# Linear attention ahead of two expert layers: one product of every third token tile moved to VectorE, one decayed copy of k left out, and the heads put together by wider products

## The chip, the cores and the metric

One core of a Trainium2 chip runs the whole program. The metric is the device time of one execution in microseconds (us); three executions of the kernel before were timed, and one more was profiled. Engines are named as in the profile: PE is TensorE's matmul, PEld its weight loads, DVE VectorE, ACT ScalarE, POOL GpSimd, SP SyncE.

## The reference

Four sequences of 768 tokens, eight heads, 48 numbers per head. A state per head takes in `k v` of each token and decays by `w`; a token also sees its own `k v`, weighted by `u`:

```python
for t in range(S):
    cur = einsum('bhd,bhe->bhde', u[None] * k[:, :, t], v[:, :, t])
    y[:, :, t] = einsum('bhd,bhde->bhe', r[:, :, t], state + cur)
    state = w[None, :, :, None] * state + einsum('bhd,bhe->bhde', k[:, :, t], v[:, :, t])
x = y.transpose(0, 2, 1, 3).reshape(B * S, H * D)      # 3072 tokens of 384
e_idx = argmax(x @ w_gate); gate_w = softmax(x @ w_gate)[e_idx]; eom = sigmoid(x @ w_output_gate)
out[e_idx == e] = gate_w * eom[:, e] * (relu(x @ w1[e]) @ w2[e])
return (silu(out @ moe2_w_gate) * (out @ moe2_w_val)) @ moe2_w_out
```

## The kernel before

The tokens are cut into 24 tiles of 128, six to a sequence. The first stage goes through the attention tile by tile; the second runs the eight experts on gathered tokens, the third the dense layer. The change is in the first stage, and in code that the kernel only branches to when a decay is out of its range (`sequential`, which does not run here).

Within a tile the decay becomes a product: `rdT` is r transposed times powers of w, `kdT` is k transposed over powers of w, and `kdc` is k by token, decayed to the tile's end. For tile i the engines do this:

- POOL, in `scaled_k(i)`: `ck` = k times u (L455), `ck` times r (L456), `kdT` (L458), `kdc` (L459). For the first three tiles the two products of `ck` are on DVE instead (L452, L453), with the intermediate in PSUM.
- DVE: `rdT` (L466), `cb`, the sum of `ck` over each head (L478), two masked copies of the scores into `dsb` (L499), the new state `st` (L527, or L522 for a sequence's first tile), and `lg`, the sum of router logits over the heads (L131).
- ACT: eight products that put `cb` on the diagonal of `dsb` (L482), the copy `yT` of the output (L556), then `xt` and `lh` out of `psx` (L126, L129).
- PE: the scores `pss` (L495), `pskv` for the state (L517, not for a sequence's sixth tile, which needs no next state), `psy` from `dsb` and v (L543) and from the state (L551), and `psx` (L124). `psx` multiplies `yT` by a table `unit`, which holds an identity and the router weights, so that one product gives x by token and the partial logits. The two heads of a pair lie in partitions 0 to 63 and 64 to 127, and a product takes 64 rows (one head) and 64 of the 128 tokens: 16 products of 64 columns per tile.

The loop `for i in range(NTILE + 3)` writes all of this out in one order, and PE, DVE, ACT, POOL and SP keep that order while it runs (their own schedules are switched off). In step i it issues `rdT` and `cb` of tile i + 1, the scores of tile i, the state of tile i - 1, `scaled_k(i + 2)`, the outputs of tile i - 1 and `psx` of tile i - 2. Between them `advance()` hands out one operation at a time of the routing of the sequence that is done (`route`, `gate`: mostly small DVE work), and `weights` splits expert weights early: `w1l` and `w2l` on DVE (L1063, 768 columns) in steps 12, 13, 15, 16, 18 and 19. Inputs come into a ring of three buffers, so `load(i + 3)` waits until DVE and POOL are done with tile i. The PSUM pools hold eight banks: `psx` has two of them, the scores two. After the loop the program works on the first expert's first tokens (`head`) while the last sequence is routed. Behind that a scheduler sets the order of the expert stage from its own estimate of times.

Of the kernel before, what the change touches and what calls it, by code (L numbers as in the profile page):

```python
# [38 lines left out]
def moe_kernel(ctx, tc, cst, small, tok, tr, u, w1, w2, m_gate, m_val, m_out, out):  # L39
# [76 lines left out]
    unit = const.tile([P, NP, 64], F32, name="unit")  # L116

    def emit(yT, x_rows, lg, pool, ps_x):
# [6 lines left out]
        xt = pool.tile([P, NP, 2, D], F32, name="xt")  # L125
        nc.scalar.copy(xt.rearrange("p q j d -> p j q d"), psx[:, :, 0:NP, 0:D])  # L126
        nc.sync.dma_start(out=x_rows, in_=xt.rearrange("p q j d -> p (q j d)"))
        lh = pool.tile([P, 2, NP, G], F32, name="lh")
        nc.scalar.copy(lh, psx[:, :, 0:NP, D:])  # L129
        yield  # L130
        nc.vector.reduce_sum(lg, lh.rearrange("p j q e -> p e (j q)"), axis=AX.X)  # L131
# [174 lines left out]
    with ExitStack() as actx:  # L306
# [111 lines left out]
        def units():  # L418
            for j in range(2):
                pr = slice(64 * j, 64 * j + 64)  # L420
                nc.gpsimd.tensor_copy(
                    unit[pr, :, 0:D],
                    ident[pr, 64 * j : 64 * j + D].rearrange("p (o d) -> p o d", o=1).to_broadcast([64, NP, D]),
                )
            nc.gpsimd.tensor_copy(unit[:, :, D:], wg[:, :, 0:G])

        S = {}
# [156 lines left out]
        def rows_out(i):  # L584
# [27 lines left out]
        with tc.manual_schedule(engines=set(engines)):  # L612
# [164 lines left out]
    def sequential(c):  # L777
# [8 lines left out]
        nc.vector.memset(ones, 1.0)  # L786
        lg = sq.tile([P, NTILE, G], F32, name="sq_lg")
        st = sq.tile([P, NP, D], F32, name="sq_st")
        with tc.For_i(0, B) as b:
            nc.vector.memset(st, 0.0)  # L790
            with tc.For_i(0, NCH) as ch:
# [709 lines left out]
```

## Time and profile before

| | |
|---|---|
| median of three executions | 829.43 us (829.01 to 830.25) |
| the profiled execution | 828.89 us, span 827.1 us, mean granted clock 0.991 |
| busy in the span | PE 790.2 us, DVE 515.1, ACT 347.6, POOL 210.6 |
| attention stage | from the start to 131.2 us, where `lg` of the last tile starts |

The span is the time from the first to the last instruction; 1.8 us of the execution lie outside of it. Busy shares are averages over stages with different limits: the attention stage must be read by itself.

### The profile page before, as it was taken

What the parts mean: (1) busy time and instruction counts of PE and PEld (TensorE: products, weight loads), DVE (VectorE), ACT (ScalarE), POOL (GpSimd) and SP (SyncE); (2) the same over time, 40 slices, a digit from 0 to 9 for tenths busy, and PEclk for the clock granted to TensorE, in tenths of its full rate; (3) what the DMA queues carried; (4) which work ended last, traced back from release to release, by engine and by line L of the source; (5) the groups of instructions that cost most, each with busy time, mean ns of one, the idle gap of its engine ahead of it and who ended that gap; (6) DMA issues with size and microseconds to landing.
All of it is one profiled execution on the core that took longest, in us unless ns stands there. A gap on an engine that the chain in (4) does not pass through costs nothing.

```text
span 827.1 us, 15617 instructions
## 1 busy us (share of the span) xinstructions
PE 790.2 (96%) x5982; PEld 718.5 (87%) x5983; DVE 515.1 (62%) x1091; ACT 347.6 (42%) x791; POOL 210.6 (25%) x207
## 2 busy tenths in 40 slices
PE   7989779699999999999999999999999999999997
PEld 4877678688999999998888888888888888889997
DVE  7789997399999999955554335333533443344443
ACT  5878663364575576554432222212222222122322
POOL 6999951354524422200001000200020020001000
PEclk9999999899999999999999999999999999999999
DMA  8899933686777877342210000000000010001000
GB/s 322 297 361 334 332 128 108 215 268 194 253 222 260 252 245 253 89 139 86 86 59 32 19 1 13 39 0 1 14 39 1 0 45 1 1 7 40 1 20 24
DMA packets 61860, 99.28 MB, mean 120 GB/s; under 512 B 5461, under 2 KB 48105, under 8 KB 61776
## 3 DMA queue, kind: packets, MB, share of 16 engines
q1 hardware_dynamic: 58320, 88.34, 32.3%
q0 software_dynamic: 3456, 9.85, 3.5%
q8 instruction: 49, 0.80, 0.4%
q14 instruction: 35, 0.29, 0.1%
HBM read 81.64 MB, written 16.53 MB: 119 GB/s over the span
## 4 chain that ended last, share of the span: by engine, by line
issue 58%; PE 16%; DVE 4%; POOL 3%; DMA 1%; ACT 1%; POOLq 0%; SPq 0%; ACTq 0%; DVEq 0%
PE ph L1188 7%; PE py L1188 6%; POOL out_dram L1332 2%; PE pya L1188 1%; DMA m<-ab 1%; PE pha L1188 1%; DVE w2l L1063 1%; PE pt L1154 1%; DVE ab L1034 1%; DMA cva<-in_w_gate_dram 0%; DVE exw L1027 0%; PE ph L1184 0%; DVE ab L1030 0%; DVE h L1208 0%; DVE low L1033 0%
## 5 line engine op out<-in xcount | busy, mean ns | idle before, releaser
L1361 DVE TENSOR_TENSOR hv<-pg,hv 128x512 f32<-128x512 f32 (+1 forms) x84 | 51.6, 615 | 153.8 <-ACT hv L1360 153.7
L1332 POOL DMA_INDIRECT out_dram<-ot,tokd x24 | 24.8, 1035 | 448.3 <-DVE ot L1331 443.6
L1360 ACT ACTIVATE hv<-pg 128x512 f32<-128x512 f32 (+1 forms) x84 | 45.1, 537 | 167.4 <-PE pg L1356 167.2
L966 ACT CAST hh<-hv 128x512 fp32r<-128x512 f32 (+1 forms) x84 | 47.0, 560 | 142.1 <-DVE hv L1362 142.1
L1323 PE MATMUL po<-wh,hl 128*128 128x384 f32 x288 | 96.8, 337 | 0.0
L1323 PE MATMUL po<-wh,hh 128*128 128x384 f32 x288 | 96.8, 336 | 0.0
L1323 PE MATMUL po<-wl,hh 128*128 128x384 f32 x288 | 96.8, 336 | 0.0
L1356 PE MATMUL pg<-xh,wh 128*128 128x512 f32 (+1 forms) x252 | 91.2, 362 | 0.0
L1356 PE MATMUL pv<-xh,wl 128*128 128x512 f32 (+1 forms) x252 | 91.1, 362 | 0.0
L1356 PE MATMUL pg<-xh,wl 128*128 128x512 f32 (+1 forms) x252 | 91.1, 361 | 0.0
L1356 PE MATMUL pv<-xh,wh 128*128 128x512 f32 (+1 forms) x252 | 91.0, 361 | 0.0
L1356 PE MATMUL pv<-xl,wh 128*128 128x512 f32 (+1 forms) x252 | 91.0, 361 | 0.0
L1356 PE MATMUL pg<-xl,wh 128*128 128x512 f32 (+1 forms) x252 | 90.7, 360 | 0.0
L1188 PE MATMUL ph<-x,w1h 128*128 128x416 f32 (+6 forms) x336 | 88.3, 344 | 0.0
L967 DVE TENSOR_TENSOR hl<-hv,hh 128x512 fp32r<-128x512 f32 (+1 forms) x84 | 51.7, 616 | 45.8 <-ACT hh L966 45.6
L1362 DVE TENSOR_TENSOR hv<-pv,hv 128x512 f32<-128x512 f32 (+1 forms) x84 | 51.7, 615 | 45.1 <-PE pv L1356 43.6
L1188 PE MATMUL py<-h,w2h 128*128 128x416 f32 (+6 forms) x336 | 79.1, 340 | 0.0
L1031 POOL TENSOR_TENSOR low<-low,exw 128x384 f32<-128x384 f32 x36 | 42.5, 1180 | 114.9 <-DVE exw L1027 73.3
L482 ACT ACTIVATE dsb<-cs,cb 128x128 f32<-128x128 f32 x192 | 58.8, 389 | 25.0 <-DVE cb L478 25.0
L1188 PE MATMUL ph<-x,w1l 128*128 128x416 f32 (+6 forms) x168 | 59.8, 356 | 3.8 <-DVE h L1208 3.1
L1188 PEld LDWEIGHTS ph<-x,w1h 128*128 128x128 f32 x336 | 62.4, 191 | 0.2
L1188 PEld LDWEIGHTS py<-h,w2h 128*128 128x128 f32 x336 | 61.0, 188 | 0.1
(244 smaller groups left out, 1699.0 us busy)
## 6 DMA issues: line engine op xcount, KB each, us to landing
r<-in_w_dram SPq DMA_DIRECT2D x64, 384.0 KB, 4.5
yd_all<-in_tr_dram SPq DMA_DIRECT2D x24, 512.0 KB, 7.5
yd_all<-in_tok_dram SPq DMA_DIRECT2D x24, 384.0 KB, 5.3
m<-ab SPq DMA_DIRECT2D x36, 192.0 KB, 3.8
rw<-m SPq DMA_DIRECT2D x36, 192.0 KB, 2.4
yd_all<-in_tok_dram SPq DMA_DIRECT2D x24, 256.0 KB, 5.9
x_d<-xt SPq DMA_DIRECT2D x24, 192.0 KB, 5.5
cva<-in_w_gate_dram SPq DMA_DIRECT2D x12, 384.0 KB, 4.3
```

What stands on the lines that cost most here:

```text
L482: nc.scalar.mul(dsb[:, h, :], ident, cb[:, h : h + 1])
L966: first = nc.scalar.copy(hi, src)
L967: second = nc.vector.tensor_tensor(out=lo, in0=src, in1=hi.bitcast(F32), op=ALU.subtract)
L1031: nc.gpsimd.tensor_tensor(out=low, in0=low, in1=ex.bitcast(F32), op=ALU.mult)
L1034: nc.vector.scalar_tensor_tensor(out=bits, in0=pair[:, :, 1], scalar=-(2**31), in1=low.bitcast(I32), op0=ALU.bitwise_and, op1=ALU.bitwise_or)
L1188: nc.tensor.matmul(dst[:, 0:n], lhsT=a, rhs=b, start=start and t == 0, stop=stop and t == 2)
L1323: mm = nc.tensor.matmul(po[t], lhsT=a[:, t * P : (t + 1) * P], rhs=bb, start=(f == 0 and j == 0), stop=(f == KF2 - 1 and j == 2))
L1332: st = nc.gpsimd.indirect_dma_start(out=out[:, :], out_offset=bass.IndirectOffsetOnAxis(ap=tokd[:, i : i + 1].bitcast(U32), axis=0), in_=o ...
L1356: nc.tensor.matmul(dst, lhsT=a[:, fs], rhs=bb[:, q, :], start=(q == 0 and j == 0), stop=(q == KD - 1 and j == 2))
L1360: nc.scalar.activation(hv, pg, AF.Sigmoid)
L1361: nc.vector.tensor_tensor(out=hv, in0=pg, in1=hv, op=ALU.mult)
L1362: nc.vector.tensor_tensor(out=hv, in0=pv, in1=hv, op=ALU.mult)
```

## The change

Three edits, all in the attention stage:

- For tiles 6, 9, 12, 15, 18 and 21 DVE does k times u, with u read from a new PSUM tile `u_ps`, which ACT fills once in step 3 (`u_table`). POOL does the second product for these tiles, `ck` times r, but now behind `kdT` and not ahead of it. The DVE product stands where `scaled_k(i)` is called, just ahead of `rdT(i)`.
- `kdc` is not made for a sequence's sixth tile (5, 11, 17 and 23).
- `unit` takes both heads of a pair into 128 rows, with zeros where a head's rows meet the other head's columns: 2 x 48 columns of x and 16 of logits. `psx` is then eight products of 128 rows, 64 tokens and 112 columns, `lh` has 64 columns per token and not 128, and `psx` needs one PSUM bank, which leaves one for `u_ps`. POOL clears the larger table (448 columns) before it copies the same pieces into it.

```diff
+    def units(unit, engine):
+        engine.memset(unit, 0.0)
+        for j in range(2):
+            pr = slice(64 * j, 64 * j + 64)
+            engine.tensor_copy(
+                unit[pr, :, j * D : (j + 1) * D],
+                ident[pr, 64 * j : 64 * j + D].rearrange("p (o d) -> p o d", o=1).to_broadcast([64, NP, D]),
+            )
+        engine.tensor_copy(unit[:, :, 2 * D :], wg[:, :, 0:G])
...
-        psx = ps_x.tile([P, 2, 8, 64], F32, name="psx", tag="x")
-        for q, (j, k) in itertools.product(range(NP), ((0, 0), (1, 1), (0, 1), (1, 0))):
-            pr, ts = slice(64 * j, 64 * j + 64), slice(64 * k, 64 * k + 64)
-            nc.tensor.matmul(psx[ts, j, q, :], lhsT=yT[pr, q, ts], rhs=unit[pr, q, :], start=True, stop=True)
+        psx = ps_x.tile([P, NP, P], F32, name="psx", tag="x")
+        for q, k in itertools.product(range(NP), range(2)):
+            ts = slice(64 * k, 64 * k + 64)
+            nc.tensor.matmul(psx[ts, q, 0 : 2 * D + G], lhsT=yT[:, q, ts], rhs=unit[:, q, :], start=True, stop=True)
...
-        nc.vector.reduce_sum(lg, lh.rearrange("p j q e -> p e (j q)"), axis=AX.X)
+        nc.vector.reduce_sum(lg, lh.rearrange("p q e -> p e q"), axis=AX.X)
...
+        def u_table():
+            t = ps_u.tile([P, NP, P], F32, name="u_ps", tag="u").rearrange("p q t -> p (q t)")[:, 0 : H * D]
+            u_ps.append(heads(t))
+            nc.scalar.copy(u_ps[0], u_tok)
...
-            else:
+            elif i < U_AT or i % U_EVERY:
                 nc.gpsimd.tensor_tensor(out=ck, in0=k_t, in1=u_tok, op=ALU.mult)
                 nc.gpsimd.tensor_tensor(out=ck, in0=ck, in1=r_t, op=ALU.mult)
+            else:
+                nc.vector.tensor_tensor(out=ck, in0=k_t, in1=u_ps[0], op=ALU.mult)
             if i:
                 nc.gpsimd.tensor_tensor(out=kdT, in0=kT, in1=wkT, op=ALU.mult)
-            nc.gpsimd.tensor_tensor(out=kdc[:, :, 0:D], in0=k_t, in1=wk_tok, op=ALU.mult)
+            if i >= U_AT and i % U_EVERY == 0:
+                nc.gpsimd.tensor_tensor(out=ck, in0=ck, in1=r_t, op=ALU.mult)
+            if (i + 1) % NCH:
+                nc.gpsimd.tensor_tensor(out=kdc[:, :, 0:D], in0=k_t, in1=wk_tok, op=ALU.mult)
...
+U_AT, U_EVERY = 6, 3
```

The first place where the order of instructions moves is POOL from tile 5 to tile 7. Before, it does four products for each tile (`ck` twice, `kdT`, `kdc`; a number behind a name is its buffer's, `yd_all` the input ring):

```order
L455 TENSOR_TENSOR ck<-yd_all 128x384
L456 TENSOR_TENSOR ck<-ck,yd_all 128x384
L458 TENSOR_TENSOR kdT<-yd_all 128x512
L459 TENSOR_TENSOR kdc_146<-yd_all 128x8x48
L455 TENSOR_TENSOR ck<-yd_all 128x384
L456 TENSOR_TENSOR ck<-ck,yd_all 128x384
L458 TENSOR_TENSOR kdT<-yd_all 128x512
L459 TENSOR_TENSOR kdc_144<-yd_all 128x8x48
L455 TENSOR_TENSOR ck<-yd_all 128x384
```

In the changed kernel the same stretch on POOL reads:

```order
L460 TENSOR_TENSOR ck<-yd_all 128x384
L461 TENSOR_TENSOR ck<-ck,yd_all 128x384
L465 TENSOR_TENSOR kdT<-yd_all 128x512 x2
L467 TENSOR_TENSOR ck<-ck,yd_all 128x384
L469 TENSOR_TENSOR kdc_147<-yd_all 128x8x48
L460 TENSOR_TENSOR ck<-yd_all 128x384
```

Tile 5's `kdc` and tile 6's first product are gone, and tile 6's second product (L467) comes after its `kdT` and waits for DVE.

The second place is DVE ahead of the sum `cb` of tile 18 (step 16), before:

```order
L527 SCALAR_TENSOR_TENSOR st_142<-st_143,yd_all,pskv 128x64 x3
L1063 TENSOR_TENSOR w2l<-r_1138,w2h 128x768
L466 TENSOR_TENSOR rdT<-yd_all,wr_ps 128x512
L478 TENSOR_REDUCE cb<-ck 128x8
L499 COPY_PREDICATED dsb<-cs,pss_1747 128x4x128
```

The same stretch of DVE in the changed kernel:

```order
L536 SCALAR_TENSOR_TENSOR st_145<-st_146,yd_all,pskv 128x64 x3
L1076 TENSOR_TENSOR w2l<-r_1071,w2h 128x768
L463 TENSOR_TENSOR ck<-yd_all,u_ps 128x384
L476 TENSOR_TENSOR rdT<-yd_all,wr_ps 128x512
L488 TENSOR_REDUCE cb<-ck 128x8
L508 COPY_PREDICATED dsb<-cs,pss_1631 128x4x128
```

The new product (L463) has only `rdT` between it and `cb`, which needs POOL's second product of the same tile; tiles 12, 15 and 21 read alike.

The third place is PE in step 3, from the state's products to the scores of tile 4, before:

```order
L517 MATMUL pskv<-yd_all,kdc_146 64x64 x8
L543 MATMUL psy<-dsb,yd_all 64x128 x8
L551 MATMUL psy<-rdT,st_142 64x128 x8
L124 MATMUL psx<-unit,yT 64x64 x16
L495 MATMUL pss_516<-rdT,kdT 128x128
```

The same stretch of PE in the changed kernel:

```order
L526 MATMUL pskv<-yd_all,kdc_149 64x64 x8
L552 MATMUL psy<-dsb,yd_all 64x128 x8
L560 MATMUL psy<-rdT,st_145 64x128 x8
L131 MATMUL psx<-unit,yT 64x112 x8
L504 MATMUL pss_506<-rdT,kdT 128x128
```

The order is the same; `psx` has half as many products, each of 112 columns, and uses 128 rows of the array where `psy<-rdT,st` just ahead of it uses 64.

Up to about 150 us of the profile nothing else moves. In the first experts' stretch behind it the scheduler has put some DVE, ACT, PE and SP rows a few places earlier or later.

## Rows read from the trace of the kernel before

**Rows 1.** Busy time by stretch: engine busy us (instructions), then PE clock, DMA share, GB/s

```profile
20.00:56.00 36.00, 32.95 (x739) 29.45 (x740) 28.60 (x82) 29.04 (x94) 35.37 (x36) 1.00 0.93 317
61.00:123.00 62.00, 51.44 (x1130) 45.44 (x1127) 59.77 (x181) 46.61 (x144) 52.66 (x47) 1.00 0.75 267
190.00:230.00 40.00, 36.90 (x191) 35.50 (x190) 38.70 (x72) 21.71 (x43) 18.81 (x14) 0.96 0.74 231
```

**Rows 2.** DVE's waits from 20 to 61 us: total, times, longest

```profile
DVE cb L478 <- POOL ck L456: 6.5, 7, 1.6
```

**Rows 3.** Timeline of POOL, the second product of tile 6 (start, us)

```profile
33.03 1.00 POOL L456 TENSOR_TENSOR ck<-ck,yd_all 128x384 f32<-128x384 f32 x1
```

**Rows 4.** Timeline of DVE, from `cb` of tile 6 to `cb` of tile 7

```profile
34.07 0.55 DVE L478 TENSOR_REDUCE cb<-ck 128x8 f32<-128x384 f32 x1 [0.81 <-POOL ck L456]
...
36.81 0.68 DVE L466 TENSOR_TENSOR rdT<-yd_all,wr_ps 128x512 f32<-128x512 f32 x1
38.32 0.55 DVE L478 TENSOR_REDUCE cb<-ck 128x8 f32<-128x384 f32 x1 [0.83 <-POOL ck L456]
```

**Rows 5.** Timeline of DVE, from the last weight split ahead of tile 18

```profile
90.09 1.75 DVE L1063 TENSOR_TENSOR w2l<-r,w2h 128x768 fp32r<-128x768 f32 x1
91.77 0.67 DVE L466 TENSOR_TENSOR rdT<-yd_all,wr_ps 128x512 f32<-128x512 f32 x1
92.37 0.54 DVE L478 TENSOR_REDUCE cb<-ck 128x8 f32<-128x384 f32 x1
```

**Rows 6.** Timeline of POOL, the second product of tile 18

```profile
86.90 1.00 POOL L456 TENSOR_TENSOR ck<-ck,yd_all 128x384 f32<-128x384 f32 x1
```

**Rows 7.** POOL's groups by line to 131 us: count, busy us, mean ns, idle

```profile
L405 POOL MEMSET yd_all<- 128x1244 f32 x1 | 1.1, 1142 | 0.0
```

**Rows 8.** Timeline of DVE, a product with one PSUM operand (tile 1)

```profile
12.26 0.56 DVE L453 TENSOR_TENSOR ck<-bank,yd_all 128x384 f32<-128x384 f32 x1
12.73 0.68 DVE L466 TENSOR_TENSOR rdT<-yd_all,wr_ps 128x512 f32<-128x512 f32 x1
```

**Rows 9.** Timeline in the expert stage, POOL released by DVE

```profile
257.39 0.35 DVE L1027 TENSOR_SCALAR exw<-ab 128x384 int32<-128x384 int32 x1
257.88 1.21 POOL L1031 TENSOR_TENSOR low<-low,exw 128x384 f32<-128x384 f32 x1 [2.58 <-DVE exw L1027]
```

**Rows 10.** Timeline of PE, from the scores of tile 4 to those of tile 5

```profile
28.35 1.16 PE L495 MATMUL pss<-rdT,kdT 64*128 64x128 f32 x16
...
29.95 1.05 PE L543 MATMUL psy<-dsb,yd_all 128*64 128x128 f32 x16
30.93 0.98 PE L551 MATMUL psy<-rdT,st 64*64 64x128 f32 x14
31.65 0.28 PE L124 MATMUL psx<-unit,yT 64*64 64x64 f32 x2
...
32.42 1.16 PE L495 MATMUL pss<-rdT,kdT 64*128 64x128 f32 x16
```

**Rows 11.** Waits of PE's weight loads from 20 to 131 us

```profile
PEld psy L551 <- issue: 3.3, 19, 0.2
```

**Rows 12.** DVE's groups by line to 131 us

```profile
L131 DVE TENSOR_REDUCE lg<-lh 128x16 f32<-128x128 f32 x23 | 8.3, 360 | 1.6 <-ACT lh L129 1.6
L1063 DVE TENSOR_TENSOR w1l<-r,w1h 128x768 fp32r<-128x768 f32 x3 | 4.8, 1601 | 0.0
L1063 DVE TENSOR_TENSOR w2l<-r,w2h 128x768 fp32r<-128x768 f32 x3 | 3.9, 1288 | 0.0
```

**Rows 13.** Timeline of DVE, a weight split behind the attention stage

```profile
138.47 0.96 DVE L1063 TENSOR_TENSOR w1l<-r,w1h 128x768 fp32r<-128x768 f32 x1
```

**Rows 14.** Timeline at the end of the attention stage: PE, then DVE

```profile
122.53 0.69 PE L517 MATMUL pskv<-yd_all,kdc 128*64 128x64 f32 x16 [1.27 <-issue]
...
131.20 0.37 DVE L131 TENSOR_REDUCE lg<-lh 128x16 f32<-128x128 f32 x1 [1.14 <-ACT lh L129]
```

**Rows 15.** PE's waits from 156 to 340 us: total, times, longest

```profile
PE ph L1188 <- DVE h L1208: 3.1, 2, 2.3
```

More of the change, by code (lines that the diff above doesn't have):

```diff
@@ L113, in moe_kernel, with emit @@
     wg = sm_t[:, 2 * NP :].rearrange("p (q g) -> p q g", q=NP)
-    unit = const.tile([P, NP, 64], F32, name="unit")
-    def emit(yT, x_rows, lg, pool, ps_x):
-        psx = ps_x.tile([P, 2, 8, 64], F32, name="psx", tag="x")
-        for q, (j, k) in itertools.product(range(NP), ((0, 0), (1, 1), (0, 1), (1, 0))):
-            pr, ts = slice(64 * j, 64 * j + 64), slice(64 * k, 64 * k + 64)
-            nc.tensor.matmul(psx[ts, j, q, :], lhsT=yT[pr, q, ts], rhs=unit[pr, q, :], start=True, stop=True)
[L125 to L129, printed above, removed]
+    def units(unit, engine):
[7 more added lines that the diff above has]
+        engine.tensor_copy(unit[:, :, 2 * D :], wg[:, :, 0:G])
+    def emit(yT, x_rows, lg, pool, ps_x, unit):
+        psx = ps_x.tile([P, NP, P], F32, name="psx", tag="x")
+        for q, k in itertools.product(range(NP), range(2)):
+            ts = slice(64 * k, 64 * k + 64)
+            nc.tensor.matmul(psx[ts, q, 0 : 2 * D + G], lhsT=yT[:, q, ts], rhs=unit[:, q, :], start=True, stop=True)
+        xt = pool.tile([P, NP, 2 * D], F32, name="xt")
+        nc.scalar.copy(xt, psx[:, :, 0 : 2 * D])
+        nc.sync.dma_start(out=x_rows, in_=xt.rearrange("p q d -> p (q d)"))
+        lh = pool.tile([P, NP, G], F32, name="lh")
+        nc.scalar.copy(lh, psx[:, :, 2 * D : 2 * D + G])
         yield
-        nc.vector.reduce_sum(lg, lh.rearrange("p j q e -> p e (j q)"), axis=AX.X)
+        nc.vector.reduce_sum(lg, lh.rearrange("p q e -> p e q"), axis=AX.X)
     counts = []
@@ L314, in moe_kernel @@
         ps_y = actx.enter_context(tc.tile_pool(name="ps_y", bufs=1, space=PSUM))
+        ps_u = actx.enter_context(tc.tile_pool(name="ps_u", bufs=1, space=PSUM))
         ps_r = actx.enter_context(tc.tile_pool(name="ps_r", bufs=1, space=PSUM))
@@ L367, in moe_kernel @@
         wk_tok = carve(H * D).rearrange("p (h d) -> p h d", d=D)
+        unit = acst.tile([P, NP, 2 * D + G], F32, name="unit")
         wr_ps = ps_c.tile([P, NP, P], F32, name="wr_ps", tag="c")
@@ L416, in tables @@
             nc.vector.tensor_copy(wide_i, wide)
[L418 to L427, printed above, removed]
+        S, u_ps = {}, []
+        def u_table():
+            t = ps_u.tile([P, NP, P], F32, name="u_ps", tag="u").rearrange("p q t -> p (q t)")[:, 0 : H * D]
+            u_ps.append(heads(t))
+            nc.scalar.copy(u_ps[0], u_tok)
         def inputs(i):
@@ L488, in scores @@
             if i == 1:
-                both = ps_x.tile([P, 2, NP, P], F32, name="pss01", tag="x")
-                pss = [both[:, j] for j in range(2)]
+                pss = [ps.tile([P, NP, P], F32, name=f"pss{j}1", tag=t) for j, (ps, t) in enumerate(((ps_x, "x"), (ps_u, "u")))]
             else:
@@ L591, in rows_out @@
             lg, mx = lgs[g.start]
-            yield from emit(S.pop(i), x_d[i * P : (i + 1) * P, :], lg[:, i - g.start, :], apool, ps_x)
+            yield from emit(S.pop(i), x_d[i * P : (i + 1) * P, :], lg[:, i - g.start, :], apool, ps_x, unit)
             if i + 1 == g.stop:
@@ L617, in moe_kernel @@
             scaled_k(1)
-            units()
+            units(unit, nc.gpsimd)
             last = iter(())
@@ L679, in moe_kernel @@
                 next(head)
-            both = ps_x.tile([P, 2, 512], F32, name="pt01", tag="x")
+            both = ps_x.tile([P, 1, 512], F32, name="pt01", tag="x")
             pts = both[:, 0, 0 : KD * P], bank[:, 0 : KD * P]
@@ L786, in sequential @@
         nc.vector.memset(ones, 1.0)
+        unit = sq.tile([P, NP, 2 * D + G], F32, name="sq_unit")
+        units(unit, nc.vector)
         lg = sq.tile([P, NTILE, G], F32, name="sq_lg")
@@ L825, in sequential @@
                 for _ in emit(
-                    yT, x_d[bass.ds(i * P, P), :], lg[:, bass.ds(i, 1), :].rearrange("p o g -> p (o g)"), sq, ps_y
+                    yT, x_d[bass.ds(i * P, P), :], lg[:, bass.ds(i, 1), :].rearrange("p o g -> p (o g)"), sq, ps_y, unit
                 ):
```

2 lines of the change are left out of this document (added).

## The prediction

> **What bounds the stage.** I read first the busy time by stretch [rows 1]. From 20 to 56 us POOL is busy for 35.37 of 36 us; from 61 to 123 us DVE is, for 59.77 of 62, and POOL no longer. So the attention stage has two halves with different bounds. The waits of DVE say the same: before 61 us it waits seven times for POOL's `ck`, 6.5 us in all [rows 2], and it has no such wait behind 56 us.
>
> Then the timeline of one tile of each half. In the first, POOL's second product of tile 6 starts at 33.03, takes 1.00, and `cb` starts 0.04 later [rows 3, 4]; from `cb` to `cb` it is 4.25 us, of which DVE waits 0.83 [rows 4]. In the second, POOL has tile 18's `ck` ready at 87.90, and DVE comes to `cb` at 92.37, 4.5 us later [rows 5, 6]: POOL is ahead, and whatever DVE is given there adds to the time. The stage's last 8.7 us are a chain of PE and ACT, from the state's products at 122.53 to `lg` at 131.20 [rows 14].
>
> **What POOL gains in the first half.** Gone by tile 11: two first products (tiles 6 and 9) and the `kdc` of tile 5, about 1.0 us each at the duration of an equal product [rows 3], so 3.0. Added: clearing 448 columns of `unit`, by a clear of 1244 columns in 1.14 us [rows 7] 0.4. If POOL set the pace alone, `cb` of tile 11 would come 2.6 earlier.
>
> It does not, because the second product now waits for DVE. The new DVE product stands where `rdT` started, 2.74 us after the last `cb` [rows 4], 2.64 with a shorter `lg` (below). It should take 0.56, as the same product with one PSUM operand did in tile 1 [rows 8]. From DVE to POOL a result needs 0.14 us (exw ends at 257.74, POOL starts at 257.88) [rows 9], POOL's product 1.00, and the way back 0.04. That is 2.64 + 0.56 + 0.14 + 1.00 + 0.04 = 4.38 us from `cb` to `cb` for such a tile, against 4.25. A DVE tile is therefore not shorter; what POOL saves is idle time ahead of the second product, and only the tile behind it gains, since `kdT` is already done. Carried on tile by tile with these pitches, `cb` comes 0.4 later at tile 5 and 0.6 later at tile 6, 0.4 earlier at tile 7, 0.5 at tile 9 and 1.2 at tile 11.
>
> **What PE takes back.** In the first half PE repeats after 4.07 us (28.35 to 32.42) [rows 10], only 0.18 under POOL's 4.25. `psy` from `dsb` puts eight products of 128 columns through in 0.98 us, on the array shape that `psx` will have, 128 rows by 64 [rows 10]; 112 columns are 0.86, against 0.77 from the start of `psx` to the next scores now. And `psx` now has the shape of its forerunner (64 rows by 64) and starts 0.72 us after it, while that one's last two are still running. When the shape changes from 128 by 64 to 64 by 64, the weight load stands still for 0.17 us, 19 times [rows 11]. The new `psx` brings such a change into each tile. The Trainium skill, TensorEngine Tiling (Array Packing), Key Properties, says that a change of the tiling mode drains TensorE, where a change of tile within a mode does not; the trace agrees, with the 0.17 us.
>
> I take 0.33 us more per tile on PE: 0.09 for the columns, 0.17 for the stop, 0.07 for lost overlap. Ends: 0.09 (no stop) and 0.45 (a stop on both sides of `psx`, with the overlap lost). At 0.33 a tile takes 4.40, and PE paces. From tile 6 on the masked copies wait for scores, and of the 1.2 us some 0.6 stay at tile 11 (all at the lower end, none at the upper).
>
> **What DVE pays in the second half.** Tiles 12, 15, 18 and 21 get a product: 0.47 us in DVE's queue (12.26 to 12.73) [rows 8]; held for its whole 0.56, it would shorten the wait below by as much. Behind it come only `rdT`, 0.60 (91.77 to 92.37) [rows 5], and then `cb`, which waits for POOL. POOL ends 0.56 + 0.14 + 1.00 + 0.04 = 1.74 after the product starts; DVE is there after 0.47 + 0.60 = 1.07. The wait is 0.67; with 0.04 for the way to POOL, as on the way back, it is 0.57. Behind the waiting `cb` on DVE stand the masked copies, for which PE waits with `psy`, and ACT's eight products wait for `cb` itself. Sum: 4 x 1.14 = 4.56 us.
>
> What DVE gets back: `lg` reads 64 columns and not 128, of a mean 360 ns [rows 12]; between 0.07 and 0.14, I take 0.10, for ten of the twelve tiles (in two DVE waits for ACT right behind it), 1.0. And the weight splits: six take 4.8 + 3.9 = 8.7 us [rows 12], while one with POOL idle takes 0.96 [rows 13]. The three `w2l` stand directly ahead of the new product, when POOL has nothing to do but wait for it; the split of 1.75 ahead of tile 18 [rows 5] falls to 0.96, and all three from 3.9 to 2.9: 1.0 gained. The `w1l` still meet POOL at work. Ends: 0, and 2.9 if all six run alone. The Trainium skill, SBUF — State Buffer, Who interferes with whom, has it that a VectorE instruction with two SBUF inputs contends with GpSimd's reads, and one with at most one SBUF input does not; the 1.75 against 0.96 agrees, and by that rule the new product with u in PSUM runs freely, as the 0.56 assumes.
>
> Net for the second half: 4.56 - 1.0 - 1.0 = 2.6 later.
>
> **The end of the stage.** In the chain from 122.53 PE does `psx` twice on the way and once more at the end: 2 x 0.33 + 0.1; the shorter `lh` and `lg` give back 0.2. So 0.5 later. At no cost I put ACT's copy of u (in step 3, where the DVE product needs it three steps on; uncovered it would cost what `xt`, as large a copy, takes once) and `kdc` of tiles 11, 17 and 23, whose POOL time is idle there.
>
> **Sum.** -0.6 + 2.6 + 0.5 = 2.5 us later at the end of attention. What follows starts from the last `lg`, so it moves along. The profiled execution took 828.89, 0.54 under the median of the three; 828.89 + 2.5 is 831.4, and against the median of 829.43 I say **831.9 us**. Runs of this kernel tell a change of about 0.2% (1.7 us) from none.
>
> **Rivals.**
> - PE pays no stop: `psx` costs 0.09 more per tile, 1.2 stays at tile 11, and the end costs 0.2: -1.2 + 2.6 + 0.2 = +1.6, 831.0. For it: no row has this change of shape itself. Against: the 19 stops. Chance 0.10 (same).
> - POOL's new idle time frees all six weight splits: 2.9 in place of 1.0, so +0.6, 830.0. Against: behind each DVE tile POOL has ten products to do, some 10 of the 15 us that DVE takes for three tiles (62 for twelve), and `w1l` comes in the second of these tiles. Chance 0.14 (same).
> - The two halves of the array do not overlap in `psx`: twice 0.86, PE at 4.07 - 0.77 + 1.72 = 5.0 us per tile against 4.25 through seven tiles, 5 us less some 1 of slack: +4 at tile 11 in place of -0.6, so 4 + 2.6 + 0.5, 836.5. Against: `psy` has this shape, and 0.98. Chance 0.08 (slower).
> - POOL still sets the pace behind tile 11: then four more products and two `kdc` count, 6.0 us, in place of DVE's 2.6: -1.2 - 6.0 + 0.5, 822.7. It decides if DVE at its `cb` waits for POOL in the second half of before; it does not [rows 6]. Chance 0.04 (faster).
> - Faster by the expert stage: its order moved a little. PE waits there 3.1 us for DVE's `h`, in two places [rows 15], and loses 4% of its clock from 190 to 230 us, 1.6 us [rows 1]. If the new order avoids both, 4.7 come off: 831.9 - 4.7 = 827.2. For it: DVE's rows around those places did move. Against: the same work meets POOL's there. It decides from 4.2 us on. Chance 0.14 (faster).
>
> **How the numbers follow.** The forecast keeps 0.50. With its own terms at their ends (wait 0.57 and `lg` 0.14, -0.8; `lg` 0.07, no split freed and PE 0.45, +0.3 + 1.0 + 0.8) it goes from 831.1 to 834.0; for the scatter of the runs 0.06 of its chance lies under the bound of 831.1. Slower 0.44 + 0.08 = 0.52; same 0.06 + 0.10 + 0.14 = 0.30; faster 0.18. The range leaves out the serial `psx`, the POOL pace and half of the last rival: 827.2 is near its lower end, so 827.6 to 834.5.
>
> **What the changed profile would show.** Right: DVE waits for POOL at `cb` of tiles 12, 15, 18 and 21, 0.6 us each, and POOL waits for DVE ahead of its second product; the DVE product at 0.56; `lg` at about 0.26; a stop of the weight load ahead of `psx`; the scores of tiles 6 to 10 late; the last `lg` at about 133.7. Wrong: no wait at those `cb`, `w1l` under 1.1, `psx` within 0.8 us, or an expert stage that does not simply move along.

## The result, and the profile after

The changed kernel took 833.13 us (median of 7 runs, 831.42 to 835.59), the kernel before 828.38 beside it (7 runs, 827.12 to 830.25): ratio 1.0053, 95% interval 1.0036 to 1.0069, so slower by 4.4 us with an interval of 3.0 to 5.7. Timed again with the experiments it was slower by 2.5 us (1.3 to 3.7). These go by the ratio on record, which is not the quotient of the two medians: the medians lie 4.75 and 3.3 us apart. The forecast was 2.5 slower.

I read the attention stage first, by the start of `cb` on DVE, and against the profile of before. At tile 11 it is 54.52 against 55.28, at tile 23 it is 118.06 against 117.31, and the last `lg` starts at 133.65 against 131.20 [rows 14]. So the first half gains 0.8, the second loses 1.5, the end loses 1.7: 2.45 in all. The span grew by 2.8 (829.9 against 827.1): in these two executions the rest moved along, but for 0.4. The rows, on DVE; before:

```profile
55.28 0.55 DVE L478 TENSOR_REDUCE cb<-ck 128x8 f32<-128x384 f32 x1 [0.47 <-POOL ck L456]
117.31 0.55 DVE L478 TENSOR_REDUCE cb<-ck 128x8 f32<-128x384 f32 x1
```

And in the changed kernel:

```profile
54.52 0.54 DVE L488 TENSOR_REDUCE cb<-ck 128x8 f32<-128x384 f32 x1
118.06 0.55 DVE L488 TENSOR_REDUCE cb<-ck 128x8 f32<-128x384 f32 x1
133.65 0.27 DVE L138 TENSOR_REDUCE lg<-lh 128x16 f32<-128x64 f32 x1 [1.47 <-ACT lh L136]
```

These are two executions. Other executions with the same code differ by up to 1.4 us at tile 23, as the experiments show, so the 2.45 is not yet the price of the change.

Busy time of the changed kernel by stretch, with the columns of [rows 1]:

```profile
20.00:56.00 36.00, 35.26 (x619) 30.69 (x621) 29.37 (x84) 29.51 (x95) 34.13 (x35) 1.00 0.93 323
61.00:123.00 62.00, 54.88 (x908) 46.68 (x903) 57.44 (x181) 46.08 (x144) 46.76 (x43) 1.00 0.76 261
190.00:230.00 40.00, 38.07 (x204) 36.64 (x203) 39.56 (x77) 22.25 (x44) 19.63 (x15) 1.00 0.72 232
```

POOL has work to spare now in both halves, and in the first PE is the busiest engine, 35.26 of 36 us. DVE is less busy in the second half than before, 57.44 against 59.77, though it was given work: the waits say why. DVE's waits of the changed kernel from 61 to 128 us (total, times, longest):

```profile
DVE cb L488 <- POOL ck L467: 2.1, 4, 0.5
DVE bank L248 <- ACT eo L244: 1.5, 3, 0.6
DVE x L980 <- ACT x L979: 1.4, 1, 1.4
```

The first row is the predicted wait, at tiles 12, 15, 18 and 21, 0.52 each. One of them on the timeline of DVE (start, duration), which answers to [rows 5]:

```profile
90.27 0.95 DVE L1076 TENSOR_TENSOR w2l<-r,w2h 128x768 fp32r<-128x768 f32 x1
91.14 0.55 DVE L463 TENSOR_TENSOR ck<-yd_all,u_ps 128x384 f32<-128x384 f32 x1
91.60 0.68 DVE L476 TENSOR_TENSOR rdT<-yd_all,wr_ps 128x512 f32<-128x512 f32 x1
92.80 0.55 DVE L488 TENSOR_REDUCE cb<-ck 128x8 f32<-128x384 f32 x1 [0.52 <-POOL ck L467]
```

POOL's side of it, on its own timeline, which answers to [rows 6]:

```profile
91.77 1.00 POOL L467 TENSOR_TENSOR ck<-ck,yd_all 128x384 f32<-128x384 f32 x1 [4.93 <-DVE ck L463]
```

POOL stood idle for 4.93 us, then did its product while DVE waited. And the weight split ahead of it, 1.75 before, takes 0.95. DVE's groups by line of the changed kernel to 133 us, which answer to [rows 12]:

```profile
L138 DVE TENSOR_REDUCE lg<-lh 128x16 f32<-128x64 f32 x23 | 5.7, 247 | 2.4 <-ACT lh L136 2.4
L1076 DVE TENSOR_TENSOR w1l<-r,w1h 128x768 fp32r<-128x768 f32 x3 | 3.7, 1228 | 0.0
L463 DVE TENSOR_TENSOR ck<-yd_all,u_ps 128x384 f32<-128x384 f32 x6 | 3.2, 542 | 0.0
L1076 DVE TENSOR_TENSOR w2l<-r,w2h 128x768 fp32r<-128x768 f32 x3 | 2.8, 943 | 0.0
```

The six splits take 6.5 us in place of 8.7: the `w2l` are freed wholly, as forecast, and the `w1l` in part, which was not. The end of the stage on PE:

```profile
123.27 0.69 PE L526 MATMUL pskv<-yd_all,kdc 128*64 128x64 f32 x16 [0.82 <-issue]
...
124.76 1.09 PE L560 MATMUL psy<-rdT,st 64*64 64x128 f32 x16
125.78 0.99 PE L131 MATMUL psx<-unit,yT 128*64 128x112 f32 x16
126.70 0.55 PE L1167 MATMUL pt<-cs,xg 128*128 128x128 f32 x3
127.72 0.52 PE L1167 MATMUL pt<-cs,xg 128*128 128x128 f32 x3 [0.47 <-DMA xg<-x_d,rows_h]
128.17 1.09 PE L552 MATMUL psy<-dsb,yd_all 128*64 128x128 f32 x16
```

Two things stand here. `psx` starts 1.02 us behind `psy` from the state, where it was 0.72 [rows 10], and needs 0.92 to its follower in place of 0.77: 0.45 more per tile, the upper end that the prediction gave. And the six transposes of gathered rows (`pt`), which stand ahead of tile 23's products in PE's queue, wait 0.47 us for a transfer. Before, all six ran without a wait:

```profile
125.50 0.87 PE L1154 MATMUL pt<-cs,xg 128*128 128x128 f32 x6
```

The stop of the weight load is seen too (waits of PE's weight loads from 20 to 123 us):

```profile
PEld psy L560 <- issue: 2.9, 17, 0.2
PEld psx L131 <- issue: 2.6, 15, 0.2
```

That is 0.17 us ahead of `psx`, as ahead of `psy` [rows 11]: a stop on both sides.

### The profile page after: what moved, and what is told of

Its sections match the earlier page's. It is cut to its first block, busy times and chain, and to the rows that moved or that the text cites. A ratio compares the mean times of both kernels' runs of the same rounds, so it can differ in the third digit from the quotient of the medians.

```text
span 829.9 us, 14843 instructions
## 1 busy us (share of the span) xinstructions
PE 799.8 (96%) x5598; PEld 722.0 (87%) x5599; DVE 513.7 (62%) x1097; ACT 347.6 (42%) x792; POOL 201.3 (24%) x198
## 4 chain that ended last, share of the span: by engine, by line
issue 57%; PE 15%; DVE 5%; POOL 3%; DMA 2%; ACT 1%; another core or an unknown queue 1%; POOLq 0%; SPq 0%; DVEq 0%; ACTq 0%
PE ph L1201 7%; PE py L1201 7%; POOL out_dram L1345 2%; DMA r<-in_w_dram 1%; DVE w2l L1076 1%; DVE w1l L1076 1%; DVE ab L1047 1%; PE pt L1167 1%; DVE ab L1043 1%; DMA m<-ab 1%; DVE h L1221 0%; DVE ab L1038 0%; DVE exw L1040 0%; ACT w1h L1073 0%
## 5 line engine op out<-in xcount | busy, mean ns | idle before, releaser
L1044 POOL TENSOR_TENSOR low<-low,exw 128x384 f32<-128x384 f32 x36 | 44.2, 1230 | 111.4 <-DVE exw L1040 81.1
L492 ACT ACTIVATE dsb<-cs,cb 128x128 f32<-128x128 f32 x192 | 58.7, 390 | 24.6 <-DVE cb L488 24.4
```

The costliest lines, as they stand in the source:

```text
L492: nc.scalar.mul(dsb[:, h, :], ident, cb[:, h : h + 1])
L1044: nc.gpsimd.tensor_tensor(out=low, in0=low, in1=ex.bitcast(F32), op=ALU.mult)
```

## The experiments

All times are medians; "over" and "under" are against the kernel before on the same chip in the same hours, by the ratio. There were three series on three chips: e1, e2, e4 and e7; e3, e5, e6 and e8; e10 to e13. The kernel before had a median of 829.22, 830.67 and 830.35 us in them, so that a ratio says more than a median, and kernels of different series are compared by it or by their traces. Intervals are at 95%.

| kernel | us | ratio to before | cb of tile 11 | last lg |
|---|---|---|---|---|
| before (profile shown above) | | | 55.28 | 131.20 |
| e1_pool_product | 830.13 | 1.0014 (1.0000 to 1.0027) | 56.07 | 132.57 |
| e2_first_half | 830.21 | 1.0011 (0.9995 to 1.0027) | 54.96 | 131.62 |
| e4_early_product | 832.54 | 1.0041 (1.0027 to 1.0056) | 55.09 | 134.35 |
| e7_delay | 834.19 | 1.0062 (1.0041 to 1.0082) | 55.26 | 132.92 |
| e3_last_four | 833.38 | 1.0023 (1.0007 to 1.0038) | 54.88 | 134.16 |
| e5_kdc_only | 829.90 | 0.9988 (0.9972 to 1.0004) | 54.16 | 130.72 |
| e6_pt_late | 832.15 | 1.0010 (0.9995 to 1.0026) | 54.74 | 132.24 |
| e8_u_sbuf | 833.18 | 1.0024 (1.0010 to 1.0039) | 54.77 | 134.02 |
| e10_before_best | 829.19 | 0.9984 (0.9968 to 1.0000) | 54.36 | 129.0 |
| e11_before_pt | 830.00 | 0.9987 (0.9971 to 1.0003) | 55.40 | 131.5 |
| e12_delay_twice | 837.33 | 1.0079 (1.0053 to 1.0105) | 54.69 | 134.92 |
| e13_after_again | 833.61 | 1.0030 (1.0016 to 1.0044) | 55.05 | 134.21 |

(For e10 and e11, where the last two `lg` stand in one row, the start of `mx` less the 0.41 that lie between them before.)

**e1_pool_product: no product by DVE at all.**

```diff
-            elif i < U_AT or i % U_EVERY:
+            else:
                 nc.gpsimd.tensor_tensor(out=ck, in0=k_t, in1=u_tok, op=ALU.mult)
                 nc.gpsimd.tensor_tensor(out=ck, in0=ck, in1=r_t, op=ALU.mult)
-            else:
-                nc.vector.tensor_tensor(out=ck, in0=k_t, in1=u_ps[0], op=ALU.mult)
```

> The changed kernel with every k*u back on POOL; the eight K=128 products of psx and the kdc that is left out for a sequence's last tile stay. Theory (the slowdown has two parts: DVE's own product and its wait in the second half, and the longer end of the stage behind the new psx): cb of tile 11 comes 0.4 to 1.0 us later than before (POOL paces again and has the clear of unit on top), the second half gains 1.0 from the shorter lg, the end costs 1.7 as in the changed kernel, so the last lg stands at 132.3 to 133.0 and the time is 1.1 to 1.8 us over the kernel before. Rival (the new psx costs nothing, all of it is DVE's product): last lg at 130.6 to 131.2, time -0.6 to 0.0. Rival (the expert stage runs longer in its new order, whatever attention does): last lg near 131 to 133 and the time still 3.5 to 4.5 us over.

The last `lg` came at 132.57 and the time 1.2 over (0.0 to 2.2), as the theory has it, so the new `psx` costs without DVE's product, if the time shows it only just. The parts: second half 60.68 us from `cb` of tile 11 to that of tile 23, against 62.03; end of the stage +1.9. The first half, 0.8 later, is no clean reading: PE's granted clock was 0.95 from 20 to 56 us in this execution, which is 1.8 us of that stretch, and from 20 to 61 us DVE waited for PE's scores six times, 5.0 us in all.

**e2_first_half and e3_last_four: DVE's product in one half alone.**

```diff
-            elif i < U_AT or i % U_EVERY:
+            elif i not in U_TILES:
...
-            if i >= U_AT and i % U_EVERY == 0:
+            if i in U_TILES:
...
-U_AT, U_EVERY = 6, 3
+U_AT, U_TILES = 6, (6, 9)
```

(In e3 `U_TILES` is 12, 15, 18 and 21.)

> The changed kernel with DVE's product at tiles 6 and 9 alone; POOL does both products of tiles 12, 15, 18 and 21. Theory (in the half that DVE paces, each such product costs time; in the half that POOL paces it does not): cb of tile 11 as in the changed kernel, 0.8 earlier than before; from there to cb of tile 23 1.0 less than before (shorter lg), where the changed kernel needs 1.5 more; end of the stage +1.7; last lg at 131.1, time within 0.5 us of the kernel before. Rival (the four products of the second half cost nothing, since DVE has idle time there or is freed of POOL in the same measure): last lg at 133.6 and the time as that of the changed kernel, 4.4 over. Rival (expert stage longer by its order): last lg at 131.1, time 2 us over.

> The changed kernel with DVE's product at tiles 12, 15, 18 and 21 alone; POOL does both products of tiles 6 and 9. Theory (the two halves add up: the first-half products gain 1.1 to 1.5 us, the second-half products cost 2.5): cb of tile 11 at 56.1 as with no DVE product at all, from there to cb of tile 23 63.2 to 63.6 us as in the changed kernel, last lg at 135.0 to 135.4, time 1.2 to 1.6 over the changed kernel. Rival (the second half costs by a state that the first half leaves, so that a late start is made up there): last lg at 133.5 and the time as that of the changed kernel.

The second half answered as said: 61.00 us without the products, 63.47 with them, the changed kernel 63.54. So the four products cost 2.5 us in the half that DVE paces, and the rival that they are free falls. (e2's time, 0.9 over with an interval of 0.4 under to 2.2 over, can't be told from that of before; it was not timed beside the changed kernel.) The first half did not answer as said: without DVE's products, e3 has `cb` of tile 11 at 54.88, the kernels with them at 54.52 to 55.09. The 1.1 to 1.5 that I had read from e1 was probably its dip of the clock: e7 and e12 had the same 0.95 there, but with the old `psx`, and were not late (55.26, 54.69), so it can have counted only where PE paces. No run of e1 without the dip shows it. The products at tiles 6 and 9 gain nothing that shows, and e3 took as long as e8, which has all six (833.38, 833.18).

**e5_kdc_only.**

```diff
-            nc.gpsimd.tensor_tensor(out=kdc[:, :, 0:D], in0=k_t, in1=wk_tok, op=ALU.mult)
+            if (i + 1) % NCH:
+                nc.gpsimd.tensor_tensor(out=kdc[:, :, 0:D], in0=k_t, in1=wk_tok, op=ALU.mult)
```

> The kernel before, with kdc left out for tiles 5, 11, 17 and 23 (whose result no later tile reads) and nothing else. Theory (only tile 5 lies in the half that POOL paces): cb of tile 7 up to 1.0 us earlier than before, of which PE's pace of 4.07 us per tile leaves 0 to 0.8 at tile 11; from tile 11 on as before; last lg 0 to 0.8 earlier, time 0 to 0.8 us under the kernel before, not to be told from it. Rival (all four count): 3 to 4 us under. Beside this it is a second look at the second half of before: the w2l of tile 18, 1.75 us in the profiled run of before, comes out near 1.0 if that run was an unlucky meeting with POOL, and the last lg is then 0.8 earlier again, at 129.6 to 130.4.

`cb` of tile 11 is 1.1 earlier, at 54.16: what the first half gains in the changed kernel is this one `kdc`, of tile 5, less what the new `psx` and its `unit` take. From there to tile 23 it is 61.28, as in e7, e11 and e12 (61.2), which keep the `kdc`, so nothing came of the other three; the rival falls. The `w2l` of tile 18 took 1.68 here too, but the second `w1l` 0.94: which split meets POOL differs by execution. The last `lg`, at 130.72, was expected earlier. Its end was 1.4 us longer than that of before, and the windows say why (columns of [rows 1]):

```profile
112.00:116.00 4.00, 2.13 (x40) 1.98 (x40) 3.90 (x14) 1.41 (x5) 0.00 (x0) 0.93 0.13 49
116.00:119.00 3.00, 3.00 (x34) 2.67 (x32) 2.59 (x11) 2.71 (x10) 0.65 (x1) 0.53 0.03 5
```

PE stood still for 1.87 us behind DVE's `sel`, and its clock fell to the lower level, 1.2 GHz, for some 3 us. Before, the same wait was 1.75 and the clock stayed at 1.00.

**e4_early_product: the wait at `cb` taken away.** DVE's product is issued behind the masked copies of the step.

```diff
+        def early_k(i):
+            if U_AT <= i < NTILE and i % U_EVERY == 0:
+                ck = S["ck", i] = apool.tile([P, H, D], F32, name="ck")
+                k_t = heads(io[i % NIO][:, RK // 2 : RK])
+                nc.vector.tensor_tensor(out=ck, in0=k_t, in1=u_ps[0], op=ALU.mult)
...
                     scores(i)
+                early_k(i + 2)
                 advance(TENSOR)
```

> The changed kernel with DVE's product issued right behind the masked copies of the step, ahead of lg and the state's update, so that POOL has its second product done when DVE comes to cb. Theory (each of the four waits of 0.52 us at cb in the second half counts in full): no wait of DVE for ck behind 61 us, second half 2.1 us shorter than in the changed kernel, last lg at 131.5, time 2.1 under the changed kernel, 2.3 over the kernel before. Rival (the product, moved ahead, makes the state's update late and PE waits for that with psy, or the masked copies wait for scores in place of cb): the wait at cb is gone, a wait of the same size stands elsewhere, the last lg stays at 133.2 to 133.6 and the time 4 over.

The theory fell, and the rival's new wait is not there either. DVE has no wait for `ck` behind 61 us, and the second half takes 63.44 us, as long as with the waits. (PE's clock fell here from 91.7 to 95.1 us; e10 and e12 had such a fall in that place too, and their halves of 61.18 and 61.24 are as long as e7's 61.22 without one.) DVE's groups of this kernel to 133 us:

```profile
L1084 DVE TENSOR_TENSOR w1l<-r,w1h 128x768 fp32r<-128x768 f32 x3 | 4.8, 1601 | 0.0
L1084 DVE TENSOR_TENSOR w2l<-r,w2h 128x768 fp32r<-128x768 f32 x3 | 4.1, 1359 | 0.0
```

The splits take 8.9 us (1.10 to 1.97 each on the timeline), 2.4 more than in the changed kernel: POOL, no longer kept waiting, works while they run. At tile 18, DVE's split and then its `cb`:

```profile
91.05 1.14 DVE L1084 TENSOR_TENSOR w2l<-r,w2h 128x768 fp32r<-128x768 f32 x1
92.11 0.68 DVE L483 TENSOR_TENSOR rdT<-yd_all,wr_ps 128x512 f32<-128x512 f32 x1
92.70 0.54 DVE L495 TENSOR_REDUCE cb<-ck 128x8 f32<-128x384 f32 x1
```

So the wait at `cb` and the free splits are one thing seen twice: POOL idle. In the timelines of all these kernels to 125 us, each split beside which POOL does nothing took 0.94 or 0.95, and the others up to 1.97. That gave the account of the second half. Take its length, from `cb` of tile 11 to that of tile 23, and subtract the six splits as they ran:

| kernels | length | six splits | rest |
|---|---|---|---|
| before | 62.03 | 8.67 | 53.36 |
| e5, e7, e10, e11, e12 (old `psx`, no product here) | 61.18 to 61.28 | 7.79 to 7.90 | 53.38 to 53.40 |
| e1, e2 (new `psx`, no product here) | 60.68, 61.00 | 7.94, 8.24 | 52.74, 52.76 |
| changed, e3, e6, e8, e13 (product, with its wait) | 63.47 to 63.54 | 6.48 to 6.53 | 56.97 to 57.02 |
| e4 (product, no wait) | 63.44 | 8.88 | 54.56 |

The rests agree within 0.05 in each class. The new `psx` with its shorter `lg` gives 0.6 back; four products cost 4.25 with their waits, 1.06 each, and 1.8 without, 0.45 each; the splits gave back 2.15 against the profile of before.

**e8_u_sbuf: is it PSUM that keeps the product short?**

```diff
-                nc.vector.tensor_tensor(out=ck, in0=k_t, in1=u_ps[0], op=ALU.mult)
+                nc.vector.tensor_tensor(out=ck, in0=k_t, in1=u_tok, op=ALU.mult)
```

> The changed kernel with DVE's product reading u from SBUF in place of PSUM; the copy into PSUM stays. In this kernel the same product of two SBUF inputs took 0.89 us (tile 0) where POOL worked beside it and 0.57 (tile 1) where POOL was idle. Theory (POOL has done kdT by then and has nothing to do but wait for this product, so nothing contends): 0.55 to 0.60 each, wait at cb 0.5 as in the changed kernel, time within 0.5 us of it. Rival (u in PSUM is what keeps the product short): 0.9 each, the wait at cb 0.85, and 0.35 later at each of tiles 12, 15, 18 and 21, 1.4 us over the changed kernel.

As the theory says: 0.54 to 0.55 each, from 61 us on. The product of tile 18 on the timeline of DVE:

```profile
91.36 0.55 DVE L463 TENSOR_TENSOR ck<-yd_all 128x384 f32<-128x384 f32 x1
```

POOL around it:

```profile
83.83 3.23 POOL L465 TENSOR_TENSOR kdT<-yd_all 128x512 f32<-128x512 f32 x2
92.00 1.00 POOL L467 TENSOR_TENSOR ck<-ck,yd_all 128x384 f32<-128x384 f32 x1 [4.93 <-DVE ck L463]
```

POOL has nothing to do while DVE multiplies, so there is nothing to meet, wherever u lies. This kernel is the changed one but for that, with its last `lg` 0.4 later, and it was 2.0 over, where the changed kernel itself was 2.5 over in the next series.

**e6_pt_late: the transposes behind tile 22's `psx`.**

```diff
-                if i == NTILE:
-                    moe.transposed(0, range(HEAD // P), ps_s, "s")
...
                     for _ in before:
                         pass
+                if i == NTILE:
+                    moe.transposed(0, range(HEAD // P), ps_s, "s")
                 weights(i, 0)
```

> The changed kernel with the six transposes of the first gathered rows put behind psx of tile 22 on PE, in place of ahead of tile 23's products. Theory (0.66 us of the longer end of the stage are those transposes, which wait 0.5 us for the gathered rows while tile 23's products stand queued behind them): the wait is gone, and so are the transposes' own 0.6 from the chain; last lg at 132.2 to 133.0, time 0.7 to 1.4 under the changed kernel. Rival (the products of the expert stage, which need the transposed rows, wait for them in turn): last lg earlier, but PE idle behind it by as much, time as that of the changed kernel.

As the theory says: last `lg` at 132.24, 14.01 us behind `cb` of tile 23 in place of 15.59, and the median 1.0 us under that of e8 beside it. The end of the stage on PE, with no wait for the gathered rows left in it:

```profile
125.95 0.99 PE L131 MATMUL psx<-unit,yT 128*64 128x112 f32 x16
126.77 1.09 PE L552 MATMUL psy<-dsb,yd_all 128*64 128x128 f32 x16
...
128.81 0.99 PE L131 MATMUL psx<-unit,yT 128*64 128x112 f32 x16
129.73 0.88 PE L1167 MATMUL pt<-cs,xg 128*128 128x128 f32 x6
130.53 0.99 PE L131 MATMUL psx<-unit,yT 128*64 128x112 f32 x16
```

**e10_before_best and e11_before_pt: what gains, without what costs.** e11 is the kernel before with the move of e6; e10 has beside it the `kdc` of e5 and DVE's product at tiles 6 and 9, with u in SBUF and the old `psx`:

```diff
+            elif i in U_TILES:
+                nc.vector.tensor_tensor(out=ck, in0=k_t, in1=u_tok, op=ALU.mult)
             else:
                 nc.gpsimd.tensor_tensor(out=ck, in0=k_t, in1=u_tok, op=ALU.mult)
```

> The kernel before (old psx), with three edits: kdc left out for tiles 5, 11, 17 and 23, k*u of tiles 6 and 9 alone done by DVE from u in SBUF, and the six transposes of the first gathered rows put behind psx of tile 22. Theory (what gains is taken, what costs is left: no product in the half that DVE paces, no new psx): cb of tile 11 at 54.0 to 55.0, from there to cb of tile 23 61.2 to 62.0 as before, the end of the stage 0.8 shorter (the transposes' PE time leaves the chain), last lg at 128.9 to 130.2, time 1.0 to 2.2 us under the kernel before. Rival (the expert stage takes back what attention gains, since its first gap of 6 us hangs on gathered rows and not on the last lg): last lg as said, time within 0.5 us of the kernel before.

> The kernel before with the six transposes put behind psx of tile 22, and nothing else. Theory: end of the stage from cb of tile 23 to the last lg 13.0 to 13.2 in place of 13.89, time 0.7 to 0.9 us under the kernel before. Rival (PE then waits for the transposed rows ahead of pha by as much): lg earlier, PE idle 0.7 longer ahead of pha, time as before.

e10 was 1.3 us under the kernel before (0.0 to 2.7), and its median 4.4 under that of the changed kernel beside it: the fastest here, though its gain on before is at the edge of what can be told, and e5 and e11 (1.0 and 1.1 under) can't be told from it. Its first half gains no more than e5's, and DVE's product of tile 9 shows a price on the timeline:

```profile
43.83 1.50 DVE L455 TENSOR_TENSOR ck<-yd_all 128x384 f32<-128x384 f32 x1
```

POOL at that time:

```profile
43.65 1.27 POOL L460 TENSOR_TENSOR kdT<-yd_all 128x512 f32<-128x512 f32 x1
```

Here POOL was at work, and the product of two SBUF inputs took 1.50 in place of 0.55. e11 was 1.1 under (0.3 over to 2.4 under; by the medians 0.35), but its last `lg` was no earlier: its PE clock fell to 0.55 from 116 to 119 us, as in e5. In e10 the end of the stage was 0.4 shorter (from `cb` of tile 23 to `mx`, 13.91 against 14.30), not the 0.7 to 0.9 expected of the move: the copies of the transposed rows now stand ahead of tile 23's `xt` on ACT and of `lg` on DVE.

**e7_delay and e12_delay_twice: does the rest move along?**

```diff
-        nc.scalar.copy(xt.rearrange("p q j d -> p j q d"), psx[:, :, 0:NP, 0:D])
+        for _ in range(6 if late else 1):
+            nc.scalar.copy(xt.rearrange("p q j d -> p j q d"), psx[:, :, 0:NP, 0:D])
```

(`late` is the last tile; eleven copies in e12.)

> The kernel before with ACT's copy xt of the last tile done six times in place of once, so that lh and the last lg come later by five copies, about 0.37 us each by their pitch: 1.85 us, last lg at 133.05. No other instruction is touched. Theory (what stands behind the last lg moves along): time 1.85 us over the kernel before, within 0.4. Rival (the expert stage has slack against its transfers, so a late lg is hidden): 0 to 0.5 over. Rival (a late lg costs more than itself, since it also puts the expert stage's order or its meetings with POOL in another place, as the medians of the changed kernel suggest, 4.75 apart with the last lg only 2.45 later): 3 to 4 over.

> The kernel before with the last tile's xt copied eleven times in place of once; with six, the last lg came 2.55 us later (five copies of 0.51) and the median rose by 5.0. Theory (what follows moves along one to one, and the 5.0 was 2.5 with the scatter of the clock's dips on top): last lg 5.1 later, time 4.5 to 6 us over the kernel before. Rival (a late lg costs twice itself): 9 to 11 over. Rival (a fixed price of 2.5 once lg is late at all, by a dip of the clock in a new gap): 7 to 8 over.

e12 was 6.5 over (4.4 to 8.7) for 5.1 of delay, which one to one allows and twice excludes; the rival of a fixed price (7 to 8) is not excluded. e7 was 5.1 over (3.4 to 6.8) for 2.55 (its copies took 0.51 each, not 0.37), more than one to one. One of PE's waits from 120 to 170 us, 0.8 us before, has grown in e7:

```profile
PE bank L171 <- DVE cum L167: 3.4, 1, 3.4
```

PE runs out of work ahead of the routing's products, 3.4 us in e7 and 5.9 in e12, and behind it the granted clock was 0.83 and 0.66 for 10 us from the last `lg`; in the kernel before and the changed one, 1.00. A bare delay is thus a worse case than the change, which adds no such gap. The profiled run of e7 was its fastest (830.92), 2.0 over that of before, so what made the others slower was not seen.

**e13_after_again: the changed kernel, unaltered.**

> The changed kernel unaltered, beside the others on one chip. In its first timing it was 4.4 us over the kernel before, [3.0, 5.7]; a kernel with the same attention stage and last lg (u read from SBUF) was 2.0 over, [0.8, 3.2]. Theory (attention's 2.45 to 2.9 is all that is lasting; what the expert stage adds is scatter that differs by occasion): 1.5 to 3.5 over, its last lg at 133.5 to 134.2. Rival (the changed kernel's expert stage is lastingly 2 us longer): 4.0 to 5.5 over.

2.5 over (1.3 to 3.7), as the theory says. The rival of a lastingly longer expert stage (4.0 to 5.5) lies outside the interval, if not far: the medians are 3.3 apart.

## Why the prediction came out as it did

**The sum was right for the two profiles, by terms that erred against each other and by some luck.** It had -0.6 + 2.6 + 0.5 = 2.5 at the last `lg`, and the profiles have -0.8 + 1.5 + 1.7 = 2.45; the `lg` foreseen at 133.7 came at 133.65. But e7, e11 and e12 run the code of before up to tile 23, and have its `cb` at 116.48, 116.61 and 115.93 where the profile of before has 117.31; the changed kernel, e13, e8 and e6 have it at 118.06 to 118.55. By the means of these four executions each, the first half gains 0.4 and the second loses 2.1; the end, 13.89 in before against 15.59 to 15.75 in the changed kernel, e13 and e8, loses 1.8. That is an estimate of 3.5 at the last `lg`, a microsecond more than forecast, and the time lay 4.4, 2.5 and 2.0 (e8) over. The profile of before was late at tile 23 for its kind, which hid much of the miss at the end of the stage.

**First half: right in size, with the gain put in the wrong place.** The prediction had DVE's tiles not shorter, and the gain behind them. Taken from `cb` of tile 5 to that of tile 11, the half has 25.2 to 25.5 us in before, e7, e11 and e12, 24.5 in e5 and e10, and 25.0 in e3 as in e2, e4, e6, e8 and e13 (24.4 in the profile of the changed kernel). So the `kdc` of tile 5 brings 0.7 to 0.9, the new `psx` takes 0.5 of it back, and DVE's products, which were two thirds of what the sum took off POOL, bring nothing that shows. (With the old `psx` and u in PSUM they were not run.) That PE would pace is borne out by its 35.26 of 36 us, and by DVE's three waits for the scores from 20 to 61 us, 1.7 us in all, of which before had none.

**Second half: each mechanism was right, three sizes were off.** The price of a product was 1.06 in place of 1.14: POOL started 0.08 behind DVE's end, not 0.14, and the wait was 0.52 for 0.67. Each `lg` is 0.11 shorter, near the 0.10 taken, but 0.6 came of it and not 1.0; what took the rest was not found. The step "the `w1l` still meet POOL" was right in part: they met it, but for less, and fell from 4.8 to 3.7 us, so that the splits gave back 2.15 and not 1.0. Some 0.8 of that is the profile of before itself, whose splits took 8.67 where five others of the old kind took 7.8 to 7.9; against those the second half lost 2.3, near the 2.6. The rival that all six splits run free was half true: 6.5, where six at 0.94 would take 5.6.

**End of the stage: the term that failed, 0.5 for 1.7.** One cause was mis-sized: `psx` costs 0.45 a tile, the stated upper end, not 0.33, and what the shorter `lh` gives back behind the last `psx` is more than eaten up by that `psx`: from its start to `lg` it is 1.71 us, 1.49 before. The other was overlooked: the transposes ahead of tile 23's products, which before held these up for 0.81 us without a wait, hold them up for 1.47, since half of them wait for the gathered rows. Followed along PE's rows, the transposes are 0.66 of the 1.7 and `psx` the rest.

With the transposes out of the way in both, the end is 14.0 in e6 and 13.5 in e10, 0.5 longer, as forecast: e10's old `psx` ends sooner, but PE then waits 0.28 for ACT's `yT`. The transposes' wait is no accident of one execution: the seven kernels with the new `psx` and the old place of the transposes all have it, 0.47 to 0.70. The second gather is issued 4.3 us behind `cb` of tile 23 in them (4.4 in before, e7 and e12), so it lands later after its issue: its transposes start 5.4 to 5.6 us behind that issue, against 4.2. Why it lands later was not shown.

**What the product's place in PSUM buys** was argued from a rule, not from this kernel's order. The Trainium skill, SBUF — State Buffer, Who interferes with whom, has a VectorE instruction with two SBUF inputs contend with a GpSimd instruction that reads SBUF. The traces agree where POOL works (1.50 in e10). They show too that in the changed kernel's order nothing hangs on it: POOL mostly waits for this very product, and u in SBUF gives 0.54 as well (e8). Where POOL does work, PSUM counts: in e4, with u in PSUM, the product of tile 6 ran wholly beside POOL's `kdT` (30.06 to 32.58), and took no longer:

```profile
31.84 0.54 DVE L450 TENSOR_TENSOR ck<-yd_all,u_ps 128x384 f32<-128x384 f32 x1
```

**The rivals.** PE without a stop: excluded by the 15 stops ahead of `psx` and the 0.45. Halves that do not overlap in `psx`: excluded, 0.99 for all of a tile's products (two rows of the profile each). POOL as the pace behind tile 11: excluded, it stands idle ahead of its product (4.93 us at tile 18). Faster by the expert stage: not so; from the last `lg` to the end it is 695.9 us before, 696.3, 697.3 and 696.3 in three profiles of the changed kernel, e13 and e8. All profiles but e12's have 695.4 to 699.0, with the old `psx` and the new.

**What stays open** is why the first timing gave 4.4 and later ones of the same attention stage 2.5 and 2.0. The medians of the changed kernel and of e8 agree (833.13, 833.61, 833.18), while those of the kernel before were 828.38 to 830.67 in four series. The three later series ran on three chips, and no kernel but before ran on more than one of these, so chip and occasion can't be told apart. The dips of the clock behind PE's waits differ from execution to execution by more than a microsecond, as e5 against before shows; that they differ by series was not shown.

## What to carry to other kernels

Before work goes from one engine to another, find the stretch in which the giver paces and the receiver does not, and give it there alone; the same edit cost 2.5 us where the receiver paces, and gained nothing that shows where a third engine was next in line. Where one engine's instructions run longer while another works, as DVE's splits did beside POOL (0.94 to 1.97 us), a wait of the one is free speed for the other, so a stall removed may come back as slower instructions; subtract such instructions from a stretch before comparing stretches. Look at what stands in the queue ahead of the last tile: here transposes that came to wait for a transfer were 0.66 of the 1.7 us lost there. And profile each kernel more than once: two executions of the same code differed by 1.4 us at tile 23, as much as the terms of the sum.

## What the runs showed of the hardware

PE's granted clock fell to 1.2 GHz inside the attention stage in some executions and not in others, behind the same kind of wait: 0.53 and 0.55 from 116 to 119 us in e5 and e11 after waits of 1.87 and 1.79 us, 1.00 before after 1.75. It made the end of the stage about 1.4 us longer each time (15.28 in e5 against 13.89 before, 14.9 in e11 against 13.5 in e10), as much as the differences that this study was to tell. A fall of the same length between 88 and 95 us, where DVE paces, cost nothing that shows (e10 and e12 beside e7). A DVE product of two SBUF inputs took 0.55 us with POOL idle and 1.50 with POOL at `kdT`, more than the whole of POOL's 1.27; with one input in PSUM it took 0.54 beside `kdT`.
